# Attention and MLP on one core: the MLP of the second 128 tokens on split half-precision weights, under another written-out order

## The chip, the cores and the metric

The kernel runs on one core of a Trainium2 chip. TensorE (PE in the profile) does the matrix products, VectorE (DVE) and ScalarE (ACT) the elementwise work, and SyncE (SP) issues the transfers, which 16 DMA engines carry. The metric is the device time of one execution in microseconds (us), median of several executions. A profiled execution also has a span, from the first to the last thing that its trace shows.

## The reference

Rotary attention over 4 batches, 8 heads, 576 tokens and head size 64, and then an MLP on all 2304 tokens:

```python
q_rot, k_rot = rotate(q), rotate(k)
scores = scale * q_rot @ k_rot.T
attn = exp(scores - max(scores)) / (sum + 1e-9)
x = (attn @ v).transpose(0, 2, 1, 3).reshape(2304, 512)
h = x @ w_in                                  # 512 -> 2048
g = where(h >= 1, h, where(h <= -1, 0, (h + 1) ** 2 / 4))
out = g @ w_out                               # 2048 -> 512
```

## The kernel before

Most products are done on half-precision parts. An f32 operand is split into a high and a low f16 half, and a product is the sum of three terms: high by high, high by low, low by high (`TERMS`). The first batch's scores and the first 128 tokens' products with v are done in plain f32, since nothing has been split yet when they run.

The attention is cut into items. An item is 128 queries of a pair of heads: score matmuls into two PSUM tiles `psS` (L669 in f32 for batch 0, L671 in halves later), two max reduces on DVE (L574), two exponentials on ACT with their sums (L576), a reciprocal (L585), and the two halves of the probabilities: the high half on ACT (L334) or DVE (L336), the low one on DVE (L599). SyncE then transposes the halves into `pT`, and PE multiplies by v (L719) into `psV`. There are 64 items, and 8 more for the last 64 tokens of each batch (L694, L697). The scores of an item need both `psS` tiles, which are free only when the item ahead has been through its two reduces and exponentials. The 72 groups of score matmuls stand in the same order before and after the change, and so one can count them.

The MLP runs in blocks of 256 tokens; the first block is cut into two units of 128 tokens, called a and b here. A step makes 512 columns of h in the one PSUM tile `psH`, ACT reads them out into `a` (L875), DVE and ACT make g of them (L870 to L885), in halves where the step runs in halves (the low half is L900), and PE multiplies g by w_out into `psO` (L893 in f32, L909 in halves). `psH` is single: the next step's first matmul (L856 in f32, L849 in halves) waits until L875 has read it. Each of the units a and b has 4 steps, a full block has 8.

The weights come in as 16 regions of 1 MB. `prep_w` puts each one together as full f32 (L518 or L520, then L521), and `halve_w` splits it into two halves in place (L334 or L336 for the high one, L539 for the low one). `SEQ` says how the steps of a and b and the four batches of splitting ("C", 4 regions each) follow each other in the program as it is planned; `WHOLE` says which of the units use the full f32 weights:

```python
WHOLE = (0, 1)
SEQ = "aabCbCabCabC"
for z in SEQ:
    if z == "C": ...            # split the next four regions
    else: next(units["ab".index(z)], None)
```

The order in which the steps are then given to the engines is a table of numbers, `ORDER`: every number takes one step out of the list of those left. The table `ON_VECTOR` says for each piece of work that either DVE or ACT can do which of them does it. Each engine works its instructions off in that order, and what waits for another engine holds up all behind it on its own.

Of the kernel before, what the change touches and what calls it, by code (L numbers as in the profile page):

```python
# [22 lines left out]


ORDER = """
# [52 lines left out]
"""  # L78


PE_LO = ()
ATT32 = (0,)
WHOLE = (0, 1)
SEQ = "aabCbCabCabC"
WIDE = 8
PE_Q1 = False
SPLIT = (0,)
F32_SCORES = 1132.0
ON_VECTOR = (
    "00000000100001000000000000000100010000001000000000000100000010001001000000000001000000001000000000100001"  # L90
    "00001000000000001100000000011000000000100000000010000000000000000000000010110100100000000000001000100000"
    "10110010100000001010100000010000100011100110000100001001000000111001000000001011111000000000100011000000"
    "10110111010100101100111101000100011010100100010111110101101001001111111001000111110100010001011101101111"
    "0001000010000110101101001110101100101101101010"
)


class Plan:


    def __init__(self):
        self.steps = []
        self.writer = {}
        self.readers = {}
        self.group = "init"
# [38 lines left out]
def kernel(  # L144
# [41 lines left out]
    pT = [sbt(f"pT{i}", [128, 18, 320], F16) for i in range(2)]  # L186
# [534 lines left out]
    def pv_group(at, j, slot, n, c0, pkeys, p0=0):  # L721
        plan.add("pe", pe_cost(14, n + 5), at, lambda: values(
            [psV[64 * a:64 * a + 64, c0:c0 + n] for a in range(2)],
            lambda a, i: pT[slot][:, 9 * (a ^ (j & 1)) + i, p0:p0 + n], j),
            r=vkeys + pkeys, w=["psV"], mode="cols")
# [41 lines left out]
                        continue  # L767
                    item(at, b, t, j, slot, c0 + 128 * i, i)
                    plan.group, plan.part = f"pv{min(b, 1)}", f"{b}{t}{j}"
                    pv_group(at, j, slot, w, w * (j % 2), [("pT", slot, i)] + ([("pT", slot, 2 + h) for h in range(2)] if i == left else []), p0)  # L770
                    if j % 2:
                        x = p0 if not last else p0 + SL * e
                        keys = [[("xT", xs, l, z, i) for z in (j - 1, j)] + ([("xL", l, e, z) for z in (j - 1, j)] if i == left else []) for l in range(2)]
# [178 lines left out]
    at = 0.0  # L952
# [134 lines left out]
```

## Time and profile before

| | us |
|---|---|
| median of 3 runs | 581.62 (580.69 to 581.66) |
| profiled execution, device time | 581.67 |
| its span | 579.45 |
| PE busy | 558.4 (96%) |
| DVE busy | 494.9 (85%) |
| ACT busy | 409.9 (71%) |

Busy is the time in which an engine had at least one instruction under way; the shares are of the span. PE's granted clock is full throughout. A share of the span is an average over stages: DVE and ACT are busier than this in the first half and less busy in the last fifth. The profiled execution is 2.2 us longer than its span and lies at the median of the runs.

### The profile page before, as it was taken

How to read it: one execution, taken by the hardware profiler on the slowest of the kernel's cores; microseconds unless marked ns; L12 is line 12 of the kernel's file. 1: busy time of each engine (PE TensorE's matmuls, PEld its weight loads, DVE VectorE, ACT ScalarE, POOL GpSimd, SP SyncE). 2: the span in 40 equal slices, each digit the busy share in tenths (PEclk: the TensorE clock that was granted, in tenths of full speed). 3: DMA queues.
4: the chain of work that ended last, by engine and by line, in shares of the span. 5: the costliest groups of instructions: out<-in, count | busy, mean ns of one | idle time of the engine just before them, and what ended most of it. 6: DMA issues, size and time to landing. Idle time of an engine off the chain costs nothing.

```text
span 579.5 us, 12028 instructions
## 1 busy us (share of the span) xinstructions
PE 558.4 (96%) x4818; PEld 373.4 (64%) x4818; DVE 494.9 (85%) x818; ACT 409.9 (71%) x800; POOL 0.7 (0%) x6
## 2 busy tenths in 40 slices
PE   4898989999999999999999999999999999999996
PEld 3566557665767576757666756666666666676673
DVE  7999989999999999999999998988999888434252
ACT  2999999999999998876777776865466655422331
POOL 0000000000000000000000000000000000000000
PEclk9999999999999999999999999999999999999999
DMA  8997999787759888976577738541865866210010
GB/s 323 388 400 253 255 258 194 175 198 188 217 106 204 155 146 170 179 173 136 114 200 115 162 60 153 93 92 47 146 100 106 140 114 131 41 38 1 2 37 18
DMA packets 172295, 87.34 MB, mean 151 GB/s; under 512 B 161168, under 2 KB 161936, under 8 KB 172240
## 3 DMA queue, kind: packets, MB, share of 16 engines
q1 hardware_dynamic: 172240, 86.59, 65.5%
q8 instruction: 37, 0.61, 0.4%
q14 instruction: 18, 0.15, 0.1%
HBM read 39.38 MB, written 4.72 MB: 76 GB/s over the span
## 4 chain that ended last, share of the span: by engine, by line
PE 69%; DVE 14%; ACT 10%; DMA 3%; issue 2%; SPq 1%; ACTq 0%; DVEq 0%
PE psO L909 25%; PE psH L849 25%; PE psV L719 7%; PE psS L671 6%; DVE sca L574 3%; DVE phl L599 2%; ACT p L576 2%; ACT phl L334 1%; ACT w L334 1%; DMA dup<-in_km_dram 1%; DVE w L539 1%; DMA pT<-phl 1%; PE psS L669 1%; ACT kT L518 1%; DVE dup L293 1%
## 5 line engine op out<-in xcount | busy, mean ns | idle before, releaser
L849 PE MATMUL psH<-xT,w 128*128 128x256 f16 (+1 forms) x1728 | 182.3, 261 | 0.7 <-ACT a L875 0.6
L909 PE MATMUL psO<-w,g 128*128 128x512 f16 x768 | 179.5, 379 | 0.0
L849 PEld LDWEIGHTS <-w 128*128 128x128 f16 x1728 | 152.1, 98 | 29.3 <-issue 1.4
L909 PEld LDWEIGHTS <-g 128*128 128x128 f16 x768 | 72.9, 98 | 74.2 <-issue 1.3
L576 ACT ACTIVATE p<-psS,sca 128x576 f32<-128x576 f32 x130 | 95.0, 733 | 26.9 <-DVE sca L574 18.3
L574 DVE TENSOR_REDUCE sca<-psS 128x1 f32<-128x576 f32 x144 | 105.6, 751 | 8.0 <-PE psS L671 4.8
L599 DVE SCALAR_TENSOR_TENSOR phl<-p,sca,phl 128x576 f16<-128x576 f32 x112 | 89.9, 812 | 4.7 <-ACT phl L334 4.0
L875 ACT ACTIVATE a<-psH 128x512 f32<-128x512 f32 x72 | 42.5, 590 | 57.1 <-PE psH L849 50.4
L878 DVE SCALAR_TENSOR_TENSOR r<-a,r 128x512 f32<-128x512 f32 x72 | 49.4, 686 | 27.5 <-ACT r L873 26.5
L334 ACT ACTIVATE phl<-p,sca 128x576 f16<-128x576 f32 x81 | 60.5, 766 | 7.9 <-DVE sca L585 6.7
L900 DVE SCALAR_TENSOR_TENSOR g<-r,g 128x512 f16<-128x512 f32 x64 | 44.0, 687 | 8.9 <-ACT g L882 7.3
L882 ACT ACTIVATE g<-r 128x512 f16<-128x512 f32 (+1 forms) x51 | 31.8, 623 | 18.1 <-DVE r L878 12.9
L671 PE MATMUL psS<-kT,qT 64*128 64x64 f16 (+1 forms) x576 | 43.7, 284 | 0.1
L671 PEld LDWEIGHTS <-qT 64*128 64x128 f16 x576 | 21.6, 94 | 30.8 <-issue 13.8
L719 PE MATMUL psV<-pT,vS 128*64 128x320 f16 (+2 forms) x512 | 40.4, 281 | 0.2
L872 ACT ACTIVATE r<-a 128x512 f32<-128x512 f32 x47 | 29.5, 627 | 7.6 <-DVE g L900 5.5
L856 PEld LDWEIGHTS psH<-xT,w 128*128 128x128 f32 x256 | 30.1, 192 | 5.5 <-issue 3.0
L856 PE MATMUL psH<-xT,w 128*128 128x128 f32 x256 | 31.7, 278 | 1.7 <-ACT a L875 1.4
L719 PEld LDWEIGHTS <-vS 128*64 128x64 f16 x512 | 25.8, 110 | 7.6 <-issue 4.6
L873 ACT ACTIVATE r<-r 128x512 f32<-128x512 f32 x47 | 29.6, 630 | 1.5
L893 PE MATMUL psO<-w,g 128*128 128x512 f32 x56 | 27.2, 611 | 2.3 <-ACT g L882 2.1
L576 ACT ACTIVATION_READ_ACCUMULATOR p<-psS,sca 128x1 f32 x130 | 25.3, 195 | 0.0
(121 smaller groups left out, 579.7 us busy)
## 6 DMA issues: line engine op xcount, KB each, us to landing
w<-in_w_in_dram SPq DMA_DIRECT2D x7, 1023.8 KB, 9.0
w<-in_w_out_dram SPq DMA_DIRECT2D x6, 1023.8 KB, 7.9
rv<-in_vm_dram SPq DMA_DIRECT2D x8, 512.0 KB, 4.6
out_dram<-o SPq DMA_DIRECT2D x16, 256.0 KB, 2.3
rk<-in_km_dram SPq DMA_DIRECT2D x6, 576.0 KB, 5.4
dup<-in_km_dram SPq DMA_DIRECT2D x6, 576.0 KB, 4.6
dup<-in_qb_dram SPq DMA_DIRECT2D x4, 640.0 KB, 4.4
rq<-in_qb_dram SPq DMA_DIRECT2D x4, 640.0 KB, 5.9
```

What stands on the lines that cost most here:

```text
L334: plan.add("act", act_cost(n), at, lambda: nc.scalar.activation(out=hi, in_=x, func=AF.Copy, scale=f), r=r, w=w)
L574: plan.add("dve", dve_cost(S, psum=True), at, lambda m=m, src=src: nc.vector.tensor_reduce(out=m, in_=src, op=ALU.max, axis=AX.X, negate=T ...
L576: plan.add("act", act_cost(S, psum=True, ptrs=2), at, lambda a=a, e=e, m=m, src=src: nc.scalar.activation(out=end_p32[e][0], in_=src, func ...
L599: plan.add("dve", dve_cost(S, ptrs=1), at, lambda a=a, e=e, hi=hi, lo=lo: nc.vector.scalar_tensor_tensor(out=lo, in0=end_p32[e][0], scalar ...
L671: nc.tensor.matmul(out=psS[a][:, lo:hi], lhsT=qT[hf][d, l, j, c:c + 128], rhs=kT[ks][d, j, m, lo:hi], start=z == 0, stop=z == 2)
L719: nc.tensor.matmul(out=outs[a], lhsT=st, rhs=moving(a, blk), start=z == 0, stop=z == len(seq) - 1)
L849: nc.tensor.matmul(out=psH[:, n * i:n * i + n], lhsT=wi[ft // 2][:, wl, kk, 128 * (ft % 2):128 * (ft % 2) + 128], rhs=xfn(xl, kk), start=z ...
L856: nc.tensor.matmul(out=psH[:, n * i:n * i + n], lhsT=w[:, kk, 128 * (ft % 2):128 * (ft % 2) + 128], rhs=x32[:, kk, :], start=kk == 0, stop ...
L875: plan.add("act", act_cost(512, psum=True, ptrs=0), at, lambda one=one: nc.scalar.activation(out=a, in_=psH, func=AF.Relu, scale=2.0 ** -7 ...
L878: plan.add("dve", dve_cost(512), at, lambda one=one: nc.vector.scalar_tensor_tensor(out=r, in0=a, scalar=one, in1=r, op0=ALU.max, op1=ALU. ...
L900: plan.add("dve", dve_cost(512), at, lambda g=g, one=one: nc.vector.scalar_tensor_tensor(out=g[:, 1], in0=r, scalar=-one, in1=g[:, 0], op0 ...
L909: nc.tensor.matmul(out=psO[pos[tt]], lhsT=g[:, gl, n * i + 128 * tt:n * i + 128 * tt + 128], rhs=wo[ft // 2][:, wl, ft % 2, :], start=ft = ...
```

## The change

Unit b, the second 128 tokens, leaves `WHOLE`. Its MLP no longer uses the full f32 weights but the split ones, in three terms: 64 matmuls of 128 columns in f32 (L856) become 192 in f16 (L849), 16 matmuls of 512 columns in f32 (L893) become 48 in f16 (L909), its x is written as two halves in place of one f32 tile, and its 4 steps get a low half of g (L900). In `SEQ` each step of b now stands behind the batch of splitting that makes its weights. `ORDER` and `ON_VECTOR` are other tables throughout. The list of keys in `pv_group` is read by the planner alone, which is not in the kernel: the order is the table's.

```diff
 ORDER = """
-2 3 0 0 24 12 7 123 122 1 16 38 1 63 1 29 18 18 2 1 20 6 33 6 2 1 1 29 0 103 0 1 0 99 25 99 3 0 97 2 96 96 0 94
+2 3 0 0 0 11 17 6 20 31 0 25 118 0 40 0 7 113 7 36 1 0 9 53 1 32 1 10 25 1 0 27 8 0 15 99 54 15 4 98 96 0 93 94
...
-WHOLE = (0, 1)
-SEQ = "aabCbCabCabC"
+WHOLE = (0,)
+SEQ = "aaCbaCbaCbCb"
...
 ON_VECTOR = (
-    "00000000100001000000000000000100010000001000000000000100000010001001000000000001000000001000000000100001"
+    "01000000000000001000000000011100100000000000000000000000000000000000000000000000100000000000000000000000"
...
-                    pv_group(at, j, slot, w, w * (j % 2), [("pT", slot, i)] + ([("pT", slot, 2 + h) for h in range(2)] if i == left else []), p0)
+                    pv_group(at, j, slot, w, w * (j % 2), [("pT", slot, z) for z in range(4)], p0)
```

The order on PE, first, at the place where the units a and b follow each other (`psO_96` takes a's output, `psO_97` b's; `xT_76` holds the x of both). Before, b's steps are f32 matmuls like a's:

```order
L893 MATMUL psO_97<-w,g_81 128x512
L856 MATMUL psH<-xT_76,w 128x128 x16
L669 MATMUL psS_92<-kT_62,qT_65 128x512
L669 MATMUL psS_93<-kT_62,qT_65 128x512
L669 MATMUL psS_92<-kT_62,qT_65 128x64
L669 MATMUL psS_93<-kT_62,qT_65 128x64
L856 MATMUL psH<-xT_76,w 128x128 x8
L893 MATMUL psO_96<-w,g_80 128x512
L856 MATMUL psH<-xT_76,w 128x128 x8
```

In the changed program b's steps are half-precision matmuls, each with its weight load, here the last of 48 of its first step and, behind a step of a, the first of its output:

```order
L849 MATMUL psH<-xT_76,w 128x128
L669 MATMUL psS_92<-kT_62,qT_65 128x512
L669 MATMUL psS_93<-kT_62,qT_65 128x512
L669 MATMUL psS_92<-kT_62,qT_65 128x64
L669 MATMUL psS_93<-kT_62,qT_65 128x64
L856 MATMUL psH<-xT_76,w 128x128 x16
L669 MATMUL psS_92<-kT_62,qT_65 128x512
L669 MATMUL psS_93<-kT_62,qT_65 128x512
L669 MATMUL psS_92<-kT_62,qT_65 128x64
L669 MATMUL psS_93<-kT_62,qT_65 128x64
L909 LDWEIGHTS g_80
L909 MATMUL psO_97<-w,g_80 128x512
```

What moved: two steps of a now stand ahead of b's first, and b's step has its split weights to wait for.

Second, ACT around the first step of the second MLP block (the ninth L875 of the program, the last row of each piece). Before:

```order
L254 ACTIVATE dup_87,sca<-rv 128x1024
L254 ACTIVATE dup_87,sca<-rvL 64x512
L334 ACTIVATE qT_65<-rq_86,sca 128x1280
L334 ACTIVATE w<-kT_63,sca 128x1024
L327 ACTIVATE o<-psO_97 128x512
L730 ACTIVATE xT_77<-psV,sca 128x320
L334 ACTIVATE kT_63<-rk,sca 128x2x576 x2
L327 ACTIVATE o<-psO_96 128x512
L875 ACTIVATE a<-psH 128x512
```

After:

```order
L576 ACTIVATE p_2_71,sca<-psS_92,sca 128x576
L576 ACTIVATE p_0_69,sca<-psS_93,sca 128x576
L580 ACTIVATE sca<-sca 128x2
L730 ACTIVATE xT_77<-psV,sca 128x320
L334 ACTIVATE qT_65<-rq_86,sca 128x1280
L334 ACTIVATE phl_73<-p_2_71,sca 128x576
L327 ACTIVATE o<-psO_96 128x512
L875 ACTIVATE a<-psH 128x512
```

What moved: the ninth L875 stood in row 188 of ACT's list and stands in row 205; two more items of attention have come ahead of it.

Third, DVE around the two max reduces of the 34th item (the last two rows of each piece), ahead of the 35th group of score matmuls. Before:

```order
L599 SCALAR_TENSOR_TENSOR phl_73<-p_2_71,sca,phl_73 128x576
L878 SCALAR_TENSOR_TENSOR r<-a,r 128x512
L599 SCALAR_TENSOR_TENSOR phl_73<-p_0_69,sca,phl_73 128x576
L585 RECIPROCAL sca<-sca 128x2
L336 TENSOR_SCALAR phl_72<-p_1_70,sca 128x576
L599 SCALAR_TENSOR_TENSOR phl_72<-p_1_70,sca,phl_72 128x576
L733 SCALAR_TENSOR_TENSOR xT_77<-psV,sca,xT_77 128x320
L278 TENSOR_SCALAR sca<-sca 128x1
L574 TENSOR_REDUCE sca<-psS_92 128x1
L574 TENSOR_REDUCE sca<-psS_93 128x1
```

After:

```order
L336 TENSOR_SCALAR phl_73<-p_0_69,sca 128x576
L583 TENSOR_SCALAR sca<-sca 128x2
L599 SCALAR_TENSOR_TENSOR phl_73<-p_0_69,sca,phl_73 128x576
L585 RECIPROCAL sca<-sca 128x2
L336 TENSOR_SCALAR phl_72<-p_2_71,sca 128x576
L900 SCALAR_TENSOR_TENSOR g_81<-r,g_81 128x512
L599 SCALAR_TENSOR_TENSOR phl_72<-p_1_70,sca,phl_72 128x576
L574 TENSOR_REDUCE sca<-psS_92 128x1
L574 TENSOR_REDUCE sca<-psS_93 128x1
```

What moved: the reduces stand in row 355 of DVE's list both before and after, but the work ahead of them is another mix, with 16 L900 in place of 12, and an L733 that stood ahead of them stands behind.

## Rows read from the trace of the kernel before

**Rows 1.** Windows: PE, PEld, DVE, ACT, POOL busy, clock, DMA share, GB/s.

```profile
20.00:147.60 127.60, 121.35 (x922) 83.03 (x918) 124.03 (x187) 121.22 (x224) 0.00 (x0) 1.00 0.91 253
20.00:233.50 213.50, 207.25 (x1710) 139.77 (x1707) 208.34 (x330) 200.38 (x384) 0.00 (x0) 1.00 0.88 216
147.60:579.40 431.80, 426.24 (x3868) 283.44 (x3860) 355.05 (x604) 281.12 (x561) 0.00 (x0) 1.00 0.58 112
```

**Rows 2.** Timeline at the second MLP block's first step: start, length, engine, instruction.

```profile
146.89 0.60 ACT L875 ACTIVATE a<-psH 128x512 f32<-128x512 f32 x1 [0.51 <-PE psH L849]
147.63 2.79 PE L849 MATMUL psH<-xT,w 128*128 128x256 f16 x24
```

**Rows 3.** Timeline at the 34th item's reduces and the 35th group of scores.

```profile
233.48 1.41 DVE L574 TENSOR_REDUCE sca<-psS 128x1 f32<-128x576 f32 x2
...
236.81 0.91 PE L671 MATMUL psS<-kT,qT 64*128 64x512 f16 x12
```

**Rows 4.** Chain that ended last, in order of time: start, length, what.

```profile
136.46 4.56 PE psO L893 x10
...
229.26 2.02 PE psV L719 x28
...
373.24 1.31 PE psH L849 x12
...
551.74 2.01 PE psH L849 x36
553.75 1.29 PE psO L909 x6
```

**Rows 5.** The page's groups of instructions: count, busy us, mean ns, idle before.

```profile
L856 PE MATMUL psH<-xT,w 128*128 128x128 f32 x256 | 31.7, 278 | 1.7 <-ACT a L875 1.4
```

**Rows 6.** ACT's groups, shapes apart: count, busy us, mean ns, idle before.

```profile
L576 ACT ACTIVATE p<-psS,sca 128x576 f32<-128x576 f32 x130 | 95.0, 733 | 26.9 <-DVE sca L574 18.3 <-DVE phl L599 4.5 <-DVE sca L583 2.2
L334 ACT ACTIVATE phl<-p,sca 128x576 f16<-128x576 f32 x81 | 60.5, 766 | 7.9 <-DVE sca L585 6.7 <-DMA pT<-phl 0.7 <-PE psS L669 0.2
...
L873 ACT ACTIVATE r<-r 128x512 f32<-128x512 f32 x47 | 29.6, 630 | 1.5
...
L576 ACT ACTIVATION_READ_ACCUMULATOR p<-psS,sca 128x1 f32 x130 | 25.3, 195 | 0.0
...
L334 ACT ACTIVATE w<-w,sca 128x1024 f16<-128x1024 f32 x13 | 14.8, 1136 | 0.2 <-DVE w L539 0.2
...
L580 ACT ACTIVATE sca<-sca 128x2 f32<-128x2 f32 x40 | 8.0, 199 | 0.6
...
L327 ACT ACTIVATE xT<-kT,sca 128x128 f32<-128x128 f32 x7 | 2.6, 397 | 0.5 <-DVE sca L585 0.5
```

**Rows 7.** DVE's groups, shapes apart, the same columns.

```profile
L574 DVE TENSOR_REDUCE sca<-psS 128x1 f32<-128x576 f32 x144 | 105.6, 751 | 8.0 <-PE psS L671 4.8 <-PE psS L697 1.5 <-ACT a L875 0.8
...
L878 DVE SCALAR_TENSOR_TENSOR r<-a,r 128x512 f32<-128x512 f32 x72 | 49.4, 686 | 27.5 <-ACT r L873 26.5
L900 DVE SCALAR_TENSOR_TENSOR g<-r,g 128x512 f16<-128x512 f32 x64 | 44.0, 687 | 8.9 <-ACT g L882 7.3
...
L336 DVE TENSOR_SCALAR phl<-p,sca 128x576 f16<-128x576 f32 x31 | 15.8, 516 | 0.6
...
L344 DVE SCALAR_TENSOR_TENSOR kT<-rk,sca,kT 128x1152 f16<-128x1152 f32 x6 | 8.4, 1412 | 0.0
...
L293 DVE TENSOR_TENSOR rk<-rk,rt 128x1152 f32<-128x1152 f32 x6 | 8.1, 1351 | 0.0
...
L306 DVE TENSOR_TENSOR rq<-rq,dup 128x1280 f32<-128x1280 f32 x3 | 4.5, 1484 | 0.0
...
L344 DVE SCALAR_TENSOR_TENSOR qT<-rq,sca,qT 128x1024 f16<-128x1024 f32 x3 | 3.8, 1276 | 0.0
...
L336 DVE TENSOR_SCALAR vS<-rv,sca 128x1024 f16<-128x1024 f32 x3 | 2.2, 744 | 0.0
```

**Rows 8.** The page's DMA issues: count, KB each, median us to landing.

```profile
w<-in_w_in_dram SPq DMA_DIRECT2D x7, 1023.8 KB, 9.0
```

More of the change, by code (lines that the diff above doesn't have):

```diff
@@ L89 @@
 ON_VECTOR = (
-    "00000000100001000000000000000100010000001000000000000100000010001001000000000001000000001000000000100001"
[L91 to L94, printed above, removed]
+    "01000000000000001000000000011100100000000000000000000000000000000000000000000000100000000000000000000000"
+    "00000100000001000000001000000100000100000010000000100000000001010000000011010100010100000100100000010010"
+    "00011000011011011100100011001010000001100010010110000000000000111100100110100101010100000011000000011010"
+    "01001100011001110000010001110100110000000000101001011010011010011011011000010100010011110010100111001101"
+    "11100110011000111010001011001111100010011010"
 )
```

102 rows, old and new, of the table ORDER are left out of this document.

## The prediction

> **What bounds the kernel now.** I read the busy time by window first, since a share of the span hides the stages. From 147.6 us on, PE is busy for 426.2 of 431.8 us; what it lacks is nearly all the last few us, where the last output is written. Between 20 and 147.6 us PE is busy for 121.4 of 127.6 us, but DVE for 124.0 and ACT for 121.2 [rows 1]. So the late kernel is bound by PE, and the early one by all three: PE's matmuls are fed by two engines that have no time left either. That is the point of this case: a cut in PE's work shortens the kernel only if DVE and ACT deliver sooner, or if what PE does behind their deliveries becomes less.
>
> Then I looked for places where PE depends on a delivery. At such a place the span is: when DVE or ACT delivers, plus all of PE's work that stands behind it in its order. The order gives what stands ahead on DVE or ACT and behind on PE, the trace gives the times. Two places show how tight it is before the change. In the timeline at the second MLP block, ACT reads the first step out of `psH` at 146.89, having waited 0.51 us for PE, and PE begins the second step at 147.63, 0.14 us after ACT's end [rows 2]. And at the 34th item, DVE begins its reduces at 233.48 and PE takes the next item's scores at 236.81, when the two exponentials between them are just done [rows 3]. Engines that meet within a us all along have no reserve for one another.
>
> **What the change removes and adds on PE.** The f32 matmul shows as two records. L856: 256 records are busy for 31.7 us, 0.124 each [rows 5]; unit b's half of them is 15.9 us. L893: ten records in a row take 4.56 us, 0.456 each [rows 4]; b's 32 take 14.6. In their place come 192 L849 of 128 columns, 36 of which take 2.01 us in a row, 0.0558 each, so 10.7 us, and 48 L909, six in 1.29 us, 0.215 each, so 10.3 us [rows 4]. PE's work falls by 30.5 - 21.0 = 9.4 us.
>
> The Trainium skill (TensorE: Matmul & The Clock Gate, "Back-to-back issue gap") speaks against this term: in streams of weight load and matmul it gives about 81 ns for 128 columns, where the isolated matmul takes about 56. By that, as an estimate, the 192 would take 15.6 us and the cut shrink to 4.5; the trace's 55.8 ns come from just such a stream of loads and matmuls, so the row decides [rows 4].
>
> All of this lies early: the second unit's MLP ends before the second block's first step in both orders. Behind the two places above PE has no f32 matmul left and none of b's to gain from. What is behind them changes by the order alone.
>
> **The first place: the second block's second step.** I counted both orders up to and with the ninth L875 of ACT. The changed one has ahead of it: 3 more L334 of 1024 columns (1.136 each, 3.4 us: weight halves that DVE made before), 3 more of 576 (0.766, 2.3), 4 more exponentials with their accumulator reads (0.733 + 0.195, 3.7: two items of attention that stood behind), 7 more L580 (0.199, 1.4), one more square in two passes (0.63 each, 1.3), and in all 3 fewer PSUM evacuations of some 0.4 (-1.2) [rows 6]. Sum 10.9. Rows in succession overlap: two reduces of 0.751 take 1.41, not 1.50 [rows 3, 7]. For 20 instructions that is up to 1.8 us; I take 1.2, since some stand behind a wait. So ACT arrives 9.7 us later: free at 146.38 before, at 156.1 now; with its 0.60 us of L875 and 0.14 us, PE starts the second step at 156.8. Behind that PE has 579.45 - 147.63 = 431.8 us left before the change; two groups of scores fewer (0.91 each) make it 430.0. Span 586.8.
>
> That lets ACT wait as much as before. Between 20 and 147.6 us it idles for 127.6 - 121.2 = 6.4 us [rows 1], and some of it was waiting for PE, which now has less to do. With none of these waits: 580.4.
>
> **The second place: the 35th group of scores.** On DVE, ahead of the 34th item's reduces: 4 more L900 (0.687 each, +2.75: unit b's low halves of g, all of them), 2 fewer L870 and L878 (-1.4), one more rotation of k and of q (1.351 + 1.484), one more L344 of 1024 columns and one fewer of 1152 (1.276 - 1.412), 3 fewer L336 of 1024 (0.744, -2.2: the weight and v halves that ACT now makes), 2 more of 576 (0.516, +1.0) [rows 7]; the short ones left, about as long as the L336 rows, come to +0.5 as an estimate. Sum +3.4, with as many instructions as before, so no overlap to take off. The reduces come at 236.9 instead of 233.48, and the scores 3.3 us behind them, at 240.2. Behind these PE had 342.6 us; it now has one product with v more (28 matmuls, 2.02), 24 more L849 of 256 columns (12 in 1.31) and 6 fewer L909 (-1.29) [rows 4], +3.4 with small ones: 346.0. Span 586.2. DVE idles for 213.5 - 208.3 = 5.2 us between 20 and 233.5 [rows 1]; with none of that, 581.0.
>
> The two places, on two engines, give 580.4 to 586.8 and 581.0 to 586.2. Of the idle time, waits for PE should go and waits of DVE and ACT for one another stay, and ACT gets more work; I take half of it: 583.6 at the first, 583.6 at the second, and 584.0 with the waits that two tight chains add to each other. PE behind these places is as busy as it can be in either case.
>
> **Edits at no cost.** The list of keys in `pv_group` is the planner's and the order is written out, so nothing waits for it. The splitting of the weights is the same work, 16 pairs; it stands earlier (the last L539 is row 186 of DVE's list and was row 209), and it is what DVE and ACT are busy with in the first window: its price is in the sums. Unit b's steps wait for it on PE; behind them stand score groups and then DVE, which is why the f32 matmuls, which needed no splitting, were worth their 9.4 us to PE in a stretch where it had to wait for the others anyway. The x of b in halves and its two L733 are among the short ones.
>
> **The rivals.**
> - PE stays the bound, and the cut lands: up to 579.45 - 9.4 = 570.0 of span, 572.3 of time. For it: PE is 96% busy, and the 19th item's reduces stand in row 197 of DVE's list, before in row 213, so the start does go faster. Against it: by the 34th item, in row 355 of both, that is spent. It decides where the 34th reduces come more than 3.4 us earlier than 233.48, as PE has that much more behind them, with 3.4 us more ahead of them on DVE: 6.8 of waits to be saved, where 5.2 are there. Chance 0.14, mostly with 576 to 580.
> - Nothing to measure: nearly all the waits that can go do go, and the places give 580.4 and 581.0 of span, 582.6 to 583.2; with an error of one us in the sums the time is within 0.2% of 581.62. Chance 0.12.
> - A new wait on SyncE: the weights are split earlier, so their loads come earlier in its list, in part ahead of the transposes for the first products with v; each is 1 MB and lands after 9.0 us [rows 8], with the DMA engines at 0.91 of their time [rows 1]. One load in the way of a transpose, or late for its L518, holds ACT and DVE for some 4 us (its share of the 253 GB/s there): 588 of span, 590 of time. Against it: among what DVE and ACT waited for before, their rows name one DMA, a transpose, for 0.7 us [rows 6, 7]. Chance 0.13.
>
> **The numbers.** The profiled execution takes 581.67, 2.2 us more than its span, and lies at the median of the runs, 581.62. So the likeliest is 584.0 + 2.2 = 586.2, slower by 0.8%; chance 0.61, with a range of its own from 582.8 to 589. A measurement of this kernel can tell about 0.2%, 1.2 us, from no change. Faster 0.14, same 0.12, slower 0.61 + 0.13 = 0.74. The range that leaves out 2 in 10 takes in the rival of no change and the top of both places with a late load: 580.3 to 590.5; out of it lie most of the faster cases and the longest waits.
>
> **What would show it.** PE's busy time near 549 us, but idle for some 20 us between 20 and 233.5 in place of 6.3 [rows 1], since by the second place its list holds that much less than the time that DVE and ACT need; DVE and ACT at 97% and more from 20 to 240 us; the ninth L875 between 150 and 156; the 34th item's reduces between 232 and 237; half as many f32 records, and a stream of 128-column matmuls at 0.056. Wrong would be the forecast if PE is busy without a gap from 100 us on: then the cut landed. And it would be wrong by its size if the sums over the lists of DVE and ACT miss by more than 2 us, or if one of the weight loads shows up as what ACT waited for.

## The result and the profile after

The changed kernel takes 589.29 us (588.52 to 591.27, 3 runs) where the kernel before takes 581.62: a ratio of 1.0144, 95% interval 1.0102 to 1.0186. Run again later beside the experiments it took 590.39 where before took 582.86, 1.0133 (1.0113 to 1.0154). So it is slower by 1.3 to 1.4%, 7.7 us; the forecast was 4.6 us. The profiled execution is a long one, 591.27 us with a span of 589.5; the profiled one of the second series has 587.9.

The two longer windows of rows 1 come first, of the profile after (PE, PEld, DVE, ACT, POOL busy, clock, DMA share, GB/s):

```profile
20.00:233.50 213.50, 199.28 (x1713) 134.55 (x1710) 203.19 (x321) 194.82 (x372) 0.00 (x0) 0.98 0.86 214
147.60:579.40 431.80, 429.25 (x3901) 286.39 (x3901) 353.81 (x607) 290.32 (x570) 0.00 (x0) 1.00 0.55 115
```

Against [rows 1], PE is idle for 14.2 us between 20 and 233.5 in place of 6.3; that it would be idle for longer was expected. But DVE is idle for 10.3 in place of 5.2 and ACT for 18.7 in place of 13.1, and that was not. The early stage has less work on PE, and all three engines wait longer in it.

The timeline at the two places of the prediction, after (start, length, engine, instruction):

```profile
158.10 0.60 ACT L875 ACTIVATE a<-psH 128x512 f32<-128x512 f32 x1 [0.36 <-PE psH L849]
158.75 0.49 PE L849 MATMUL psH<-xT,w 128*128 128x256 f16 x3
...
240.82 1.42 DVE L574 TENSOR_REDUCE sca<-psS 128x1 f32<-128x576 f32 x2
...
243.91 0.91 PE L671 MATMUL psS<-kT,qT 64*128 64x512 f16 x12
```

These answer to [rows 2, 3]. The ninth L875 comes 11.2 us later than before (146.89) and the 34th item's reduces 7.3 us later (233.48). Behind the start of the second step the span of 589.47 has 430.7 us left, behind the 35th scores 345.6; forecast were 430.0 and 346.0. So nearly the whole miss lies ahead of the places.

What the engines wait for between 20 and 160 us, after: for ACT, then DVE, then SyncE's queue (us in total, times, longest):

```profile
ACT kT L518 <- DMA w<-in_w_in_dram: 1.8, 1, 1.8
...
ACT kT L518 <- DMA rv<-in_w_out_dram: 1.5, 1, 1.5
ACT phl L334 <- DMA pT<-phl: 1.3, 2, 1.2
...
DVE w L521 <- ACT kT L518: 4.0, 5, 1.5
...
SPq L245 <- DVE w L521: 18.1, 6, 5.3
```

L518 is the first step of putting a raw weight together, and it waits for its load; L521 on DVE waits for L518. The queue of SyncE in turn holds the next load (L245) until L521 has freed the region that it goes to, 18.1 us in all, and what is behind it in that queue, transposes among it, waits as well. Before, in the same stretch, L518 waits once for a load, and the queue's wait is half as long:

```profile
ACT kT L518 <- DMA w<-in_w_in_dram: 0.9, 1, 0.9
...
SPq L245 <- DVE w L521: 9.0, 5, 4.1
```

The chain that ended last, between 60 and 100 us of the profile after, goes through these transfers (start, length, what):

```profile
63.40 16.49 DMA pT<-phl x2
...
86.81 7.46 DMA rv<-in_w_out_dram
```

Two transposes in a row and a weight load are 24 of the 40 us. This looks like what the third rival said, a late load or a transpose behind one; the experiments put a price on it. The prediction gave it as an alternative; here it is there beside the rest.

Groups of instructions on PE, shapes apart, after (count, busy us, mean ns, idle before):

```profile
L909 PE MATMUL psO<-w,g 128*128 128x512 f16 x816 | 191.5, 379 | 0.3 <-DVE g L900 0.2
...
L849 PE MATMUL psH<-xT,w 128*128 128x128 f16 x576 | 35.4, 219 | 1.3 <-DVE xT L733 0.6 <-ACT xT L730 0.5 <-ACT a L875 0.2
...
L856 PE MATMUL psH<-xT,w 128*128 128x128 f32 x128 | 17.3, 296 | 0.7 <-ACT a L875 0.5 <-ACT xT L327 0.2
```

Of the groups that grew, before:

```profile
L909 PE MATMUL psO<-w,g 128*128 128x512 f16 x768 | 179.5, 379 | 0.0
...
L849 PE MATMUL psH<-xT,w 128*128 128x128 f16 x384 | 23.9, 219 | 0.0
```

Half of the MLP's f32 matmuls are gone. L856 falls from 31.7 us [rows 5] to 17.3, while b's halves add 11.5 us to L849 of 128 columns and 12.0 to L909.

### The profile page after: what moved, and what is told of

Read it like the earlier page. It is cut to its first block, busy times and chain, and to the rows that moved or that the text cites. A ratio compares the mean times of both kernels' runs of the same rounds, so it can differ in the third digit from the quotient of the medians.

```text
span 589.5 us, 12183 instructions
## 1 busy us (share of the span) xinstructions
PE 561.6 (95%) x4898; PEld 374.7 (64%) x4898; DVE 491.4 (83%) x818; ACT 418.7 (71%) x812; POOL 0.7 (0%) x6
## 4 chain that ended last, share of the span: by engine, by line
PE 67%; DVE 15%; DMA 7%; ACT 6%; issue 3%; SPq 1%; ACTq 0%; DVEq 0%
PE psO L909 26%; PE psH L849 25%; PE psV L719 7%; PE psS L671 6%; DMA pT<-phl 4%; DVE sca L574 4%; DVE phl L599 3%; DMA w<-in_w_in_dram 1%; DVE w L539 1%; DMA rv<-in_w_out_dram 1%; ACT p L576 1%; DVE r L878 1%; DVE rk L293 1%; DVE g L900 1%; PE psS L697 1%
## 5 line engine op out<-in xcount | busy, mean ns | idle before, releaser
L849 PE MATMUL psH<-xT,w 128*128 128x256 f16 (+1 forms) x1920 | 194.5, 257 | 1.5 <-DVE xT L733 0.6
L909 PE MATMUL psO<-w,g 128*128 128x512 f16 x816 | 191.5, 379 | 0.3 <-DVE g L900 0.2
L849 PEld LDWEIGHTS <-w 128*128 128x128 f16 x1920 | 162.8, 98 | 31.6 <-issue 3.2
L909 PEld LDWEIGHTS <-g 128*128 128x128 f16 x816 | 77.4, 98 | 79.8 <-DVE g L900 1.5
L599 DVE SCALAR_TENSOR_TENSOR phl<-p,sca,phl 128x576 f16<-128x576 f32 x112 | 90.5, 812 | 5.7 <-ACT phl L334 5.1
L875 ACT ACTIVATE a<-psH 128x512 f32<-128x512 f32 x72 | 42.6, 592 | 54.2 <-PE psH L849 45.8
L334 ACT ACTIVATE phl<-p,sca 128x576 f16<-128x576 f32 x82 | 61.5, 767 | 12.6 <-DVE sca L585 5.6
L900 DVE SCALAR_TENSOR_TENSOR g<-r,g 128x512 f16<-128x512 f32 x68 | 46.7, 687 | 9.4 <-ACT g L882 7.6
L872 ACT ACTIVATE r<-a 128x512 f32<-128x512 f32 x53 | 33.2, 626 | 7.0 <-DVE g L900 6.2
L873 ACT ACTIVATE r<-r 128x512 f32<-128x512 f32 x53 | 33.4, 630 | 1.7
L719 PEld LDWEIGHTS <-vS 128*64 128x64 f16 x512 | 25.7, 109 | 10.7 <-issue 8.0
L669 PE MATMUL psS<-kT,qT 64*128 64x512 f32 (+1 forms) x128 | 27.3, 450 | 4.9 <-ACT p L576 4.4
L669 PEld LDWEIGHTS psS<-kT,qT 64*128 64x128 f32 x128 | 14.2, 188 | 19.4 <-ACT p L576 9.7
L719 PE MATMUL psV<-pT,vM 128*64 128x320 f16 (+2 forms) x320 | 23.9, 279 | 0.0
```

What stands on the lines that cost most here:

```text
L334: plan.add("act", act_cost(n), at, lambda: nc.scalar.activation(out=hi, in_=x, func=AF.Copy, scale=f), r=r, w=w)
L599: plan.add("dve", dve_cost(S, ptrs=1), at, lambda a=a, e=e, hi=hi, lo=lo: nc.vector.scalar_tensor_tensor(out=lo, in0=end_p32[e][0], scalar ...
L669: nc.tensor.matmul(out=psS[a][:, lo:hi], lhsT=qF[hf][d, j, c:c + 128], rhs=kF[d, j, lo:hi], start=True, stop=True)
L719: nc.tensor.matmul(out=outs[a], lhsT=st, rhs=moving(a, blk), start=z == 0, stop=z == len(seq) - 1)
L849: nc.tensor.matmul(out=psH[:, n * i:n * i + n], lhsT=wi[ft // 2][:, wl, kk, 128 * (ft % 2):128 * (ft % 2) + 128], rhs=xfn(xl, kk), start=z ...
L875: plan.add("act", act_cost(512, psum=True, ptrs=0), at, lambda one=one: nc.scalar.activation(out=a, in_=psH, func=AF.Relu, scale=2.0 ** -7 ...
```

## The experiments

Each run is compared by its ratio to the kernel before, run in turn on the same chip, since that one's median lay between 581.49 and 582.9 in the four series. One per cent is 5.8 us.

The expectations name four theories. By the TensorE theory, PE's work counts wherever it lies. By the pace theory, DVE and ACT, with what they wait for, set the first 240 us, and PE's work there counts for little or nothing. By the transfer theory, late weight loads cause the loss. By the order theory, the new order causes it, and not the halves as such.

**The changed kernel again**, as a base for the rest.

> The changed kernel itself, unaltered, run beside the others so that they have a base on the same chip: 588 to 592 us by every theory.

590.39 us, 1.0133.

**More and less work on PE.** In one run the first matmuls of b are done twice, in another b has one term of three:

```diff
-for z, (kk, wl, xl) in enumerate(seq):
+for z, (kk, wl, xl) in [y for _ in range(2 if blk == 1 else 1) for y in enumerate(seq)]:
```

> The changed kernel, with the first matmuls of unit b (L849 into psH, 192 of 128 columns) run a second time over the same bank, so the result is the same and TensorE does about 10.7 us more between 100 and 200 us. Pace theory: 0 to 3 us more than the changed kernel (589 to 592), because these matmuls fit in TensorE's idle 14.2 us or push its backlog by less than their own length only if they stand behind the last late arrival. TensorE theory: the whole 10.7, about 600. If granted clock dips from idling are part of the loss, a little less than 589.

593.84 us, 1.0193 (1.0170 to 1.0216): 0.6% above the changed kernel, 3.5 us of the 10.7 that PE did more (the group of L849 of 128 columns goes from 35.4 to 46.2 us), a little above what the pace theory gave and far from the TensorE theory.

```diff
-seq = [(kk, wl, xl) for kk in range(KT) for wl, xl in TERMS]
+seq = [(kk, wl, xl) for kk in range(KT) for wl, xl in (TERMS[:1] if blk == 1 else TERMS)]
...
-for z, (gl, wl) in enumerate(TERMS):
+for z, (gl, wl) in enumerate(TERMS[:1] if blk == 1 else TERMS):
...
```

> The changed kernel, with one term in place of three in both matmul groups of unit b, so that its 128 rows are right to half precision only: 128 matmuls of 128 columns and 32 of 512 are left out, by 55.8 ns and 215 ns about 14.0 us of TensorE between 100 and 240 us. Pace theory: 0 to 2 us less than the changed kernel. TensorE theory: the 14 us less. If TensorE's work is late at the second place (the run with more of it on TensorE took about 3 us longer), up to 4 less.

591.36 us, 1.0161 (1.0136 to 1.0187): nothing gained from 14 us less; if anything 0.3% lost. From 20 us to the ninth L875, behind which hardly any work of b is left, PE is busy for 118.7 us where the changed kernel (second series) has 124.2, so only 5.5 of the 14 us appear as shorter busy time. The granted clock goes with that (windows of this run):

```profile
60.00:100.00 40.00, 32.52 (x244) 20.12 (x243) 37.41 (x53) 37.32 (x65) 0.00 (x0) 0.86 0.97 231
100.00:150.00 50.00, 41.84 (x280) 25.48 (x280) 45.76 (x65) 46.50 (x90) 0.00 (x0) 0.84 0.77 162
```

The clock is 0.86 and 0.84 of full in these stretches, where PE is busy for 81% and 84% of the time; in the changed kernel it is 0.91 and 1.00. The 5.5 us that remain bring the end no nearer. Work that PE is spared in this stage of the changed kernel is worth nothing.

**The same on the kernel before.** Here b's f32 matmuls into `psH` are done twice:

```diff
-for kk in range(KT):
+for kk in list(range(KT)) * (2 if blk == 1 else 1):
```

> The kernel before, with the f32 matmuls L856 of unit b run a second time over the same bank (same result): 64 matmuls of about 0.25 us, 15.9 us more of TensorE between 95 and 200 us, where TensorE was idle 6.3 us. Pace theory: 2 to 8 us more than before, if f32 work in this stage is as cheap as its removal was worthless. TensorE theory: 10 to 16 more.

594.62 us, 1.022 (1.0195 to 1.0245): 12.8 us of the 15.9 by the ratio, 11.8 by the medians. That is what the TensorE theory gave, and the pace theory as I put it misses here. PE is busy for the whole of the 140 us from 100 to 240 (139.6 before, where the profile shows 0.4 us of idle time), and ACT's eighth L875 waits 2.97 us for L856. In the kernel before, PE had so little room that more work made it the engine that is late; it doesn't follow that less work would have gained as much.

**More work on DVE.** Every second low half of the weights is written twice:

```diff
-plan.add("dve", dve_cost(1024, ptrs=1), at, lambda: nc.vector.scalar_tensor_tensor(
-    out=lo, in0=y, scalar=f, in1=hi, op0=ALU.mult, op1=ALU.subtract),
+plan.add("dve", dve_cost(1024, ptrs=1), at, lambda: [nc.vector.scalar_tensor_tensor(
+    out=lo, in0=y, scalar=f, in1=hi, op0=ALU.mult, op1=ALU.subtract) for _ in range(1 + i % 2)],
```

> The changed kernel, with the low half of every second weight tile (L539, 8 of 16, 1.277 us each) written twice with the same values: DVE does 10.2 us more between about 60 and 200 us. Pace theory: 8 to 10 us more than the changed kernel (597 to 600), since DVE is late all the way to the 34th item. TensorE theory: 0 to 2. Transfer theory (DVE only waits for weight loads): 3 to 7, since its 10.3 us of idle time would take part of it up.

597.37 us, 1.0257 (1.0232 to 1.0282): 7.2 us more than the changed kernel for 10.2 us of work, 70%, where PE's extra work counted by 33%. Somewhat below what the pace theory gave.

**Less work on DVE.** Unit b's low halves of g are left out:

```diff
-plan.add("dve", dve_cost(512), at, lambda g=g, one=one: nc.vector.scalar_tensor_tensor(
+plan.add("dve", dve_cost(512), at, lambda g=g, one=one: None if blk == 1 else nc.vector.scalar_tensor_tensor(
...
-nc.tensor.matmul(out=psO[pos[tt]], lhsT=g[:, gl, n * i + 128 * tt:n * i + 128 * tt + 128],
+nc.tensor.matmul(out=psO[pos[tt]], lhsT=g[:, 0 if blk == 1 else gl, n * i + 128 * tt:n * i + 128 * tt + 128],
...
```

> The changed kernel without unit b's four subtractions L900 on DVE (4 of 0.686 us, 2.75 in all); its second matmuls read the high half in their place, so that term of b is not the reference's. TensorE does what it did. Pace theory: 2 to 3 us less than the changed kernel. TensorE theory: 0. Transfer theory: 0 to 1.

590.07 us, 1.0135 (1.0104 to 1.0165): no difference, with a spread from 586.95 to 593.36, too wide to exclude 2 us by this run alone. This went against my theory: 2.75 us of the 3.4 that I had put on DVE's list are these four instructions.

**The transfers.** Nine of the raw weight loads bring half of their columns, first in the changed kernel and then, as the control, in the kernel before:

```diff
-dma(at, raw[:, 0:4095], (w_out if which else w_in).bitcast(U16)[c][:, 1:4096], [], rk_, 128 * 8192)
+end = 2047 if 4 <= i < 13 else 4095
+dma(at, raw[:, 0:end], (w_out if which else w_in).bitcast(U16)[c][:, 1:end + 1], [], rk_, 128 * 8192)
```

> The changed kernel, with nine of its sixteen raw weight loads (the fifth to the thirteenth) bringing only half of their columns; the other half keeps what an earlier load left there, so half of those weights are not the reference's. About 4.7 MB less are moved between 45 and 100 us. Transfer theory: 3 to 5 us less than the changed kernel (584 to 586). Pace theory with late loads as no part of it: 0 to 1 less.

586.56 us, 1.0067 (1.0046 to 1.0088): 0.66% less than the changed kernel, 3.8 us.

> The kernel before, with the same nine raw weight loads (the fifth to the thirteenth) bringing only half of their columns, so half of those weights are not the reference's. Transfer theory (the changed order makes loads late that were not late before): 0 to 1 us less than before, against the 4 that the same cut was worth in the changed kernel. If the loads cost both kernels the same, 3 to 5 less, and the transfers do not explain the difference between the two.

581.2 us where before took 582.22, 0.9986 (0.9969 to 1.0004): no difference that can be told, at most 1.8 us. The same cut in the same loads is worth 3.8 us in one order and 0.8 in the other. So the size of these loads costs time in the changed order alone. The windows from 20 to 100 us show whom they held up, of the changed kernel (second series) and then of the one with half loads:

```profile
20.00:100.00 80.00, 72.13 (x556) 49.94 (x552) 75.24 (x116) 75.91 (x144) 0.00 (x0) 0.94 0.93 285
```

```profile
20.00:100.00 80.00, 71.56 (x590) 50.32 (x589) 78.72 (x120) 79.00 (x153) 0.00 (x0) 0.98 0.80 230
```

With half loads DVE is busy for 78.7 of the 80 us and ACT for 79.0, against 75.2 and 75.9: some 3 us of waiting on either engine are gone, and PE's busy time hardly differs. The chain says the same. Between 45 and 100 us of the changed kernel (second series) it has these three transfers in it, 24 of 55 us, and with half loads none (in the kernel before one, a load of k of 7.7 us):

```profile
49.75 7.88 DMA w<-in_w_in_dram
...
69.03 9.29 DMA pT<-phl
...
85.47 6.78 DMA rv<-in_w_out_dram
```

The run doesn't tell the late load apart from the transpose that is slowed by it; both get shorter. But one thing it does tell: the queue's wait for L521 (L522 in this run's kernel) is still there between 20 and 160 us,

```profile
SPq L245 <- DVE w L522: 17.6, 6, 5.2
```

while ACT and DVE no longer wait for any transfer in that stretch, where ACT did for 5.0 us in the first profile and 3.0 in the second series. So this wait of the queue does not cost the 3.8 us by itself; they go when the transfers arrive in time.

**Both cuts at once**, to see whether the late loads only hid the price of the low halves; the edits are the two shown above.

> The changed kernel with both cuts at once: nine raw weight loads bring half of their columns, and unit b's four subtractions L900 are left out, so half of those weights and one term of b are not the reference's. Alone the first took about 4 us off and the second nothing. If DVE's longer list is a price of its own and only the late loads hid it: 2 to 3 us below the run with half loads, a ratio to before of 1.002 to 1.004. If the low halves of b are off the path anyway: the same as with half loads, 1.006 to 1.008.

586.33 us where before took 581.49, 1.0079 (1.0064 to 1.0094): the same as with half loads alone. The low halves of b are off the path either way.

**Halves in the order of before.** I took before's order and put b's steps behind the split weights that they read. In the code only `WHOLE`, `SEQ` and the two tables differ from before.

> The order of before is kept on every engine; only unit b goes over to halves, and its steps are put behind the split weights that they read. Pace theory (DVE and ACT, with what they wait for, set the first 240 us, and TensorE work saved there is worth nothing): the ninth low-half subtraction and the four of b cost DVE about 3 us, the 9.4 us of TensorE are not seen; 582 to 588 us. TensorE theory (its work counts wherever it lies): 572 to 576. Order theory (the loss of the changed kernel comes from its new order alone): 580 to 583, that is, within 0.2% of before.

649.79 us, 1.1151. None of the theories meant that. The order is a bad one: between 85 and 245 us PE waits 22 us for ACT's exponentials, ACT 13.9 us for PE's products with v, and each queue stands behind a step that isn't ready. Products with v also stand behind transposes into the same columns, so they read later items' values; the amount of work is the same. The run says nothing of halves as such.

**Two orders made by a search.** The steps were moved about within their dependences, to shorten the time of a simple model of the engines, once for b in halves and once for b in f32.

> The changed kernel's program with the same engines for every step and another order: a search over a simple model of the engines (steps moved within their dependences) made it, starting from the changed order. If halves as such cost time (low halves on DVE, the wait for the split weights): still 584 us or more. If the loss of the changed kernel is the order's (loads, splits and attention standing badly for one another): under 584, and down to 575 if PE's saved work counts once DVE and ACT are fed without waits.

> The kernel before, unit b in f32, put through the same search from its own order. Order theory: it gains less than the halves do, 0 to 7 us, so that the two end within 2 us of one another. If f32 is better as such in this stage, it stays 5 us or more below the reordered halves.

613.25 us, 1.0544 (1.0516 to 1.0572), and 613.7 us, 1.0534 (1.0494 to 1.0573). Only `ORDER` differs from the changed kernel and from the one before. Both expectations are missed by far, so the model has left out something that decides; what it is stays open. Two things can be said: with orders from the same search, halves and f32 can't be told apart, and an order moves the time by 5% with the same work in it.

## Why the prediction was right, and where its size was not

All runs of either order (not those of the three other orders) can be laid side by side by the time of the first place (start of the ninth L875) and the second one (start of the 34th item's reduces) in their profiles:

| profile | first place | second place | span | span behind the first | span behind the second |
|---|---|---|---|---|---|
| before | 146.89 | 233.48 | 579.5 | 432.6 | 346.0 |
| before, half loads | 146.47 | 233.05 | 579.4 | 432.9 | 346.4 |
| before, f32 twice | 161.44 | 248.15 | 594.1 | 432.7 | 346.0 |
| changed | 158.10 | 240.82 | 589.5 | 431.4 | 348.7 |
| changed, second series | 156.22 | 239.14 | 587.9 | 431.7 | 348.8 |
| PE more | 161.53 | 243.06 | 592.2 | 430.7 | 349.1 |
| PE less | 158.65 | 240.16 | 588.8 | 430.2 | 348.6 |
| DVE more | 163.54 | 246.00 | 595.0 | 431.5 | 349.0 |
| no low half | 160.25 | 242.92 | 591.6 | 431.4 | 348.7 |
| half loads | 154.79 | 237.23 | 586.0 | 431.2 | 348.8 |
| half loads, no low half | 154.33 | 236.98 | 585.6 | 431.3 | 348.6 |

The two columns on the right hardly move within one order, whatever was added or taken away, while the first place moves by 15 us in the one order and 9 in the other. That is the main claim of the prediction, borne out by eleven profiles: the span is the time at which the early stage delivers, plus what PE has behind it. Which engine sets that time, the table doesn't say.

- **"What is behind them changes by the order alone"**: right. Behind the first place it is 1.6 us less than before on the mean of the rows of the changed order (431.1 against 432.7; forecast 1.8), behind the second one 2.7 more (348.8 against 346.1). The forecast of 3.4 more was counted from the 35th scores, and there it measured 2.9 in the changed kernel's first profile. The prediction has b's MLP end before the second block's first step; in the changed order its last three L909 (0.8 us) stand between the first and the second step, which changes nothing here.
- **PE's work, -9.4 us**: the mechanism right, the size off and without effect. By the busy time of their groups b's halves cost 23.5 us and the f32 groups fell by 27.9 (14.4 of L856, 13.5 of L893, whose two groups fall from 31.1 to 17.6), so 4.4 less. Half of the f32 groups of before is 31.4 us; the other 3.5 us are a's f32 matmuls, which got longer. The lower clock goes with that: the scores L669, the same work, take 27.3 us where they took 23.8. PE's whole busy time rose from 558.4 to 561.6 us instead of falling to 549. That less work on PE is worth nothing in the changed kernel's early stage is shown by the run with 14 us less of it.
- **The back-to-back rule**: the Trainium skill (TensorE: Matmul & The Clock Gate, "Back-to-back issue gap") gives about 81 ns where a weight load goes with each matmul of 128 columns; by that, as an estimate, the 192 would have added 15.6 us. They added 11.5, 60 ns each, near the row's 55.8.
- **ACT 9.7 us later at the first place**: right in kind, 2.2 us too long. The prediction counted from the program's start. From there ACT's busy time up to the ninth L875 is 128.1 us before and 135.6 and 135.7 in the two profiles of the changed kernel, 7.5 more. The lengths of the added rows come to 10.5, about the 10.9 counted, but the overlap of rows in succession takes 3.0 off and not 1.2. (From 20 us on the difference is 9.1, since by then ACT has done 1.5 us less than before.)
- **DVE's +3.4 us at the second place**: mis-sized, and its largest piece of no effect. The lengths of the rows do come to 3.3, but DVE's busy time up to the 34th reduces is 224.1 us before and 225.4 after, 1.3 more: DVE has 357 instructions ahead of them before and 361 after, not as many as before, and they overlap. The two runs without 2.75 of it are no faster. That the forecast of 236.9 for the reduces agrees with the 237.23 of half loads is no proof of it: the second place simply follows the first by 81.5 to 82.9 us in every changed run.
- **"I take half of it"**, the waits of DVE and ACT that should go: this is the term that was mis-sized most, by its sign. From 20 us to the first place ACT idles for 6.4 us before and for 6.6 (second series) to 8.5 (first profile) after; from the program's start it is 18.8 before and 20.5 to 22.5 after. The prediction took 3.2 off. With no waits gone, its first place gave 586.8 us of span, 589.0 of time, which is what was measured; but that is in part luck, as a list 2.2 us too long made up for 1.7 to 3.7 us of longer idle time. Nor did the old waits stay: ACT's wait in L334 for the reciprocals L585 between 20 and 160 us falls from 1.7 us to 0.2, and waits for transfers, 5.0 us after (1.8, 1.5, 1.3 and 0.4; 3.0 in the second series) against one of 0.9 us before, took their place.
- **The third rival**, SyncE's new wait: it had a chance of 0.13 and a price of 4 us, and late transfers did come at about that price, though the queue's own wait stayed at 17.6 us when they no longer were late. Halving the loads takes off 3.8 us in the changed order and 0.8, which can't be told from nothing, in the old one. The mistake was to list it as another way that it could go. It doesn't exclude the main case, it adds to it. With the loads halved in both kernels the changed one is still slower by 1.0067 / 0.9986 = 1.0081, 4.7 us, and the forecast was 4.6; with a list 2.2 us shorter than counted and no idle time saved, the agreement is luck in part.
- **The first rival**, PE stays the bound and the cut lands: shown wrong for the changed order by the run with less work on PE. It is half right for the kernel before, where more PE work counts by 80%; no run took work off PE there.
- **What should show**: PE idle 14.2 us up to 233.5 in place of some 20; DVE and ACT busy for 95% and 91% from 20 to 240 and not 97, ACT having been at 94% before; the ninth L875 at 156.2 to 158.1 and not by 156; the reduces at 239.1 to 240.8 and not by 237. The last three miss on the side of longer waits, as the prediction's last sentence on what would show it said of a weight load that ACT waits for; PE is idle for less than forecast because its work shrank by less.

What stays open is the 4.7 us that are left with half loads. With the loads halved in both kernels the first place comes at 154.79 in place of 146.47, 8.3 us later; up to it, from the program's start, ACT's busy time is 6.8 us longer and its idle time 1.5. So ACT's longer list is long enough for the rest. But DVE's list up to the same place is longer too, by 6.3 us, and right ahead of the place in the changed kernel's first profile ACT waits 1.58 us for PE's product with v (L730) and PE 1.45 us for DVE's L599. Writing more on DVE counts by 70%; no run took work off ACT, and none gave back the old table of who does what (`ON_VECTOR`). That the longer lists make the 4.7 us is argued from the rows, not shown, and the two lists can't be told apart. A transfer of transposes that takes 6.5 us at 185 us stands in the chain of the changed kernel and with half loads, and not in that of before; no run moved it.

## What to carry to other kernels

Where several engines have hardly any idle time in a stage, don't count work taken off one of them as gain: here 14 us off PE and 2.75 off DVE were worth nothing in the changed order, while work put on PE or DVE cost a third to four fifths of its length. Find the delivery on which everything behind depends, count what stands ahead of it in each engine's list, with the overlap of its instructions, and don't write off the idle time in that list as gain. When weights are prepared earlier so that a faster product can use them, their loads and the release of the buffers that they land in move too; see which engine then waits for a transfer, and make the transfer shorter to price it. And a rival that can happen together with the main case belongs in its sum, not beside it.

## What was not expected of the hardware

The granted clock fell in stretches of the early stage, where PE had less to do. Before, it is full in every window; after, these stretches among others show less, in windows of 5 us of the first profile:

```profile
30.00:35.00 5.00, 4.98 (x27) 4.25 (x27) 4.74 (x15) 5.00 (x7) 0.00 (x0) 0.67 1.02 413
...
75.00:80.00 5.00, 4.70 (x14) 1.73 (x13) 4.14 (x7) 4.42 (x8) 0.00 (x0) 0.66 1.08 179
```

PE's level was down to 1.2 GHz for part of each, while PE was busy for nearly all of the first and 94% of the second; in the 10 us ahead of the first it had been busy for 8.65, where before it was for 9.49. Less work did not always lower it: from 140 to 155 us PE was busy for 11.6 of the 15 us, and the clock was full there and behind. What decides it these runs don't show. With 14 us less work on PE the clock was at 0.84 from 100 to 150 us, and 8.5 of the 14 us did not show as shorter busy time. So here a part of the work that PE was spared came back as slower work; whether that costs the kernel anything no run tells, since less time on PE in this stage is worth so little.
